# Ten smaller places for left operands and six raw places, from the first SwiGLU layer on

## The chip, the core and the metric

The kernel runs on one core of a Trainium2 chip. The time is the device time of one execution in microseconds. The engines that matter here are TensorE (PE in the profile, its weight loads PEld), VectorE (DVE), ScalarE (ACT), GpSimd (POOL) and SyncE (SP). Each follows its own list of instructions in order and waits on semaphores for the others. SP does nothing but issue transfers; POOL also issues some.

## The reference

```python
xn = _layernorm(x)                      # x: 1 x 2048 x 1024, float32
q, k, v = split_heads(xn @ wqkv)        # 32 heads of 32
pq, pk = phi(q), phi(k)                 # t + 1 where t > 0, else exp(t); + 1e-6
kv = einsum("bhsd,bhse->bhde", pk, v)
num = einsum("bhqd,bhde->bhqe", pq, kv)
den = einsum("bhqd,bhd->bhq", pq, pk.sum over s) + 1e-6
s = merge_heads(num / den) @ wo
h = silu(xn @ w1) * (xn @ w3)           # 2048 x 3584
g = silu(h @ w2)                        # w2: 3584 x 1024
return x + s * g
```

The change touches the two products at the end: the out-projection that gives `s`, and `h @ w2`, which is summed over 3584 columns of h.

## The kernel before, in words

Both products are done by blocks with seven products in place of eight (a Strassen form). Each float32 operand is split into a high part, rounded to the type that TensorE takes, and a low part, the rest. A product is then three matmuls: high by high (L103), high by low (L104) and low by high (L105). They are recorded at those lines whatever layer they belong to.

A `Segment` is one matrix product over all 2048 rows. Six of them run one after the other in the last third of the kernel: the attention's out-projection `s` (four k-steps), then five layers `B0` to `B4` that each take a part of the 3584 columns (`FB`: two k-steps in B0, three in the others; a k-step is 2 × 128 columns). Layers add to the accumulators `acc`, which stay in the on-chip memory; `uB` is a running sum that is stored in `u_d` between layers. In the last layer `finish` applies Silu (ACT, L1331), multiplies by `ss` (the attention's `s`, DVE, L1332), adds the input `xs` for some blocks (DVE, L1334) and stores the block.

A segment goes over eight row groups m = 0 to 7 of 256 rows. Each row group needs seven left operands, in this order: A11, S2, S3, S1, A12, A22, S4 (for the products B11, T2, T3, T1, B21, T4, B22). The left operands of the B layers lie in device memory in `h_d`. One goes through these steps:

- SP issues a load of its float32 form into a raw place (`left`, L1262 in the trace; the tile is called r..., for instance rS2B). A load is 128 KB in B0 and 192 KB in B1 to B4.
- ACT casts it to the high part of the operand's tile (XS2B, `split`, L95).
- DVE subtracts the high part from the raw form, which gives the low part (L96). After that the raw place is free for the next load.
- PE uses high and low part; after the last matmul that uses it, the operand's place is free.

The right operands (B11, T2 and so on, called B_k and T_k in the order of the program) are loaded and split by the same two lines L95 and L96 and kept for a whole layer. Their raw places are others.

In row groups m=1 to m=6 the kernel does one product after the other over all k-steps, in four banks of the matmul's accumulation memory (`aB` to `dB`). In m=0, and in m=7 if a layer follows, the k-steps are outermost and the seven products have a bank each, named for the product (B11B, T2B and so on), so that the right operands of the next layer can arrive k-step by k-step. At a seam between two layers, therefore, all seven left operands of m=7 are held until its end.

The order on each engine is made by a scheduler, from the program and from the places that a tile pool has; a pool with more places lets an operand's steps be put earlier. Before, all left operands of the attention and of the layers lie in pool `pb`, eight places of 4 KB per partition, and their raw forms in four places of 2 KB (tag `sg` of pool `pc`). Both pools live through the whole kernel. `era2` is a group of pools on the other (right) side of the memory that is closed when the attention is done; pool `pw`, with the right operands and the accumulators, opens in its room.

Of the kernel before, what the change touches and what calls it, by code (L numbers as in the profile page):

```python
# [9 lines left out]
F32 = mybir.dt.float32  # L10
FR = mybir.dt.float32r
# [5 lines left out]
P = 128  # L17
C = 512
# [4 lines left out]
def tile_linear_attention_times_swiglu(  # L23
# [67 lines left out]
    def split(pair, src, bias=None):  # L91

        hi, lo = pair[:, 0], pair[:, 1]
        if bias is None:
            nc.scalar.copy(out=hi, in_=src)  # L95
            return nc.vector.tensor_sub(out=lo, in0=src, in1=hi.bitcast(F32))  # L96
        nc.scalar.activation(hi, src, AF.Identity, bias=bias)
        return nc.vector.scalar_tensor_tensor(lo, src, bias, hi.bitcast(F32), op0=ALU.add, op1=ALU.subtract)
# [6 lines left out]
        return nc.tensor.matmul(acc, lhsT=wl, rhs=ah, start=False, stop=stop, skip_group_check=True)  # L105


    pb = ctx.enter_context(tc.tile_pool(name="pb", bufs=8))
    pe = ctx.enter_context(tc.tile_pool(name="pe", bufs=3))
    pc = ctx.enter_context(tc.tile_pool(name="pc", bufs=6))  # L110
    era1, era2 = ExitStack(), ExitStack()
    ctx.enter_context(tc.tile_pool(name="edge", bufs=1, side="right")).tile([P, 8], F32, name="edge")
    pa = era2.enter_context(tc.tile_pool(name="pa", bufs=1, side="right"))
    praw = era1.enter_context(tc.tile_pool(name="praw", bufs=2))
    st = era1.enter_context(tc.tile_pool(name="st", bufs=2))
# [2 lines left out]
        return pc.tile([P, C], F32, tag="c", name=name)  # L118

    def signed(name):  # L120
        return pc.tile([P, C], F32, tag="sg", bufs=4, name=name)

    def job_tile(shape, name):
        return praw.tile(shape, F32, tag="job", bufs=4, name=name)
# [66 lines left out]
    class Opening:  # L191
# [27 lines left out]
        def run(self):  # L219
            for step in OPENING.split(";"):  # L220
                name, *args = step.split()
                done = getattr(self, "do_" + name)(*args)
                if done is not None:
                    last = done
            return last
# [274 lines left out]
    def in_turn(groups):  # L500

        done = object()
        for g in groups:
            left = [o.stages for o in g]
            while left:
                for made in list(left):
                    if next(made, done) is done:
                        left.remove(made)
                    else:
                        yield  # L510
# [132 lines left out]
    def key_rows(h, pair):  # L643
# [7 lines left out]
        def steps(n, c, src):  # L651
            j = 2 * pair + n
            pk = signed(f"pk{h}_{j}_{c}")
            z = st.tile([P, 1], F32, tag="z", name="z")
            yield from phi_steps(src, pk, z)
            nc.vector.scalar_tensor_tensor(zacc[:, j:j + 1], z, C * 1e-6, zacc[:, j:j + 1],
                                           op0=ALU.add, op1=ALU.add)
            later.append([3, lambda: turn(n, c, pk)])
# [92 lines left out]
    def row_sums(i, m, b, u, v):  # L751
        V = nc.vector

        def keep(n, t):
            nc.gpsimd.dma_start(out=g_d[n][:, m], in_=t)

        if i == 0:
            u[m] = signed(f"gu{m}")
            nc.scalar.copy(out=u[m], in_=b)
        elif i == 2:  # L760
            V.tensor_add(out=u[m], in0=b, in1=u[m])
        elif i == 3:
            v[m] = pe.tile([P, C], F32, tag="u", name=f"gv{m}") if m else st.tile([P, C], F32, tag="own", bufs=1, name="gv")
            V.tensor_sub(out=v[m], in0=b, in1=u[m])
        else:
            c = small(f"gc{i}_{m}")
            if i == 1:
                nc.scalar.copy(out=c, in_=b)
            elif i == 4:
                V.tensor_sub(out=c, in0=v[m], in1=b)  # L770
            elif i == 5:
                V.tensor_add(out=c, in0=b, in1=u[m])
            else:
                V.tensor_sub(out=c, in0=v[m], in1=b)
            keep({1: 2, 4: 1, 5: 3, 6: 0}[i], c)

    def half(h):
# [13 lines left out]
        def queries(pair, **how):  # L791

            def use_q(n, c, src):
                j = 2 * pair + n
                pq = signed(f"pq{h}_{j}_{c}")
                phi(src, pq)
                nc.gpsimd.dma_start(out=pq_d[j // JG][2 * h + c][:, j % JG], in_=pq)  # L797

            return gemm(ops[f"q{h}_{pair}_"], A, use_q, **how)
# [327 lines left out]
    class Segment:  # L1127


        def __init__(self, name, nk, first, last, place, right, left, acc, end=None):  # L1130
            self.last, self.U = last, {}
            self.name, self.nk, self.first = name, nk, first
            self.place, self.right_of, self.left_of, self.acc, self.end = place, right, left, acc, end
            self.Y, self.X = {}, {}
# [9 lines left out]
        def operands(self, m):  # L1144

            self.X[m] = {}
            if not self.first:

                self.U[m] = pe.tile([P, C], F32, tag="u", name=f"u{self.name}_{m}")
                nc.sync.dma_start(out=self.U[m], in_=u_d[m])  # L1150
            for n, src in self.left_of(m):
                self.X[m][n] = pb.tile([P, 2, self.nk, P], FR, tag="b", name=f"X{n}{self.name}_{m}")
                split(self.X[m][n], src)

        def product(self, b, X, n, ks, start=True):
# [90 lines left out]
                take(c12, bd)  # L1246
                end(0, 1)

    loads = []

    def left(m, src, nk, name, first=False):

        big = None
        for e, n in enumerate(PRODUCTS):
            n = PARTNER[n]
            if first:
                if e % 2 == 0:
                    big = job_tile([P, 2, nk, P], f"r{e}{name}_{m}")
                t = big[:, e % 2]
            else:  # L1260
                t = signed(f"r{n}{name}_{m}")[:, :nk * P].rearrange("p (k s) -> p k s", s=P)
            loads[:] = [nc.sync.dma_start(out=t, in_=src(n))]  # L1262
            if name == "q" and m < 2:

                fetched[:] = loads
            yield n, t
# [15 lines left out]
    def second_weights(i, n, k):  # L1282
        if (i, n, k) not in asked:
            ask(i, n, k, small)
        return asked[i, n, k]
# [109 lines left out]
    def layer_place(n, i, k):  # L1395
# [4 lines left out]
                      lambda n, _, k, i=i: second_weights(i, n, k),  # L1400
# [6 lines left out]
            layers[0].right(0, [i for i in range(7) if i * 5 // 7 == m - 2])  # L1407

    run(attention, ahead=ask_next, around=first_weights)
    layers[0].operands(0)  # L1410
    era2.close()
    pw.append(ctx.enter_context(tc.tile_pool(name="pw", bufs=1, side="right", reuse_waits="tile")))
    for k in range(1, layers[0].nk):
        layers[0].right(k)
# [27 lines left out]
```

## Time and profile before

| | us |
|---|---|
| median of 3 runs | 2333.54 (2331.86 to 2333.63) |
| profiled execution | 2329.57 |
| its span | 2327.8 |
| PE busy in the span | 2288.8 (98%) |
| DVE busy | 1773.8 (76%) |
| ACT busy | 927.4 (40%) |
| POOL busy | 686.7 (30%) |
| last matmul of the attention starts | 1778.44 |
| first matmul of B0 starts | 1778.66 |

The profile is of one execution. Its times are microseconds from the span's start. Rows of a timeline give the start, the duration, the engine, the line, the operation, output and inputs, and in brackets the idle time of the engine ahead of it with what ended it. Matmuls are pipelined: each takes 0.39 us in the record, but the next one starts 0.23 us after it. The granted TensorE clock in the profiled execution is 0.999 of full speed.

### The profile page before, as it was taken

The page shows a single profiled execution, that of the slowest core. Times are in us where ns is not written, and L with a number is a line of the kernel's source. Part 1 is how long each engine was busy: PE and PEld are TensorE (multiplying, and loading weights), DVE is VectorE, ACT ScalarE, POOL GpSimd, SP SyncE. Part 2 cuts the span into 40 slices and gives each one's busy share as a digit, 9 for nine tenths or more (in the row PEclk, how much of TensorE's full clock was granted, in tenths as well). Part 3 has the DMA queues.
Part 4 walks back from the last instruction along what each step waited for, and adds up shares of the span by engine and source line. Part 5 has one row for each costly group of instructions (what it writes and reads, how often), then busy time and mean ns, then how long its engine had stood idle before and what let it go on. Part 6 is the DMA issues. An engine that isn't in the chain of part 4 may idle for free.

```text
span 2327.8 us, 31758 instructions
## 1 busy us (share of the span) xinstructions
PE 2288.8 (98%) x10752; PEld 1873.8 (80%) x10752; DVE 1773.8 (76%) x2820; ACT 927.4 (40%) x1645; POOL 686.7 (30%) x851
## 2 busy tenths in 40 slices
PE   6999999999999999999999999999999999999998
PEld 5888888888887888777887888888888888888876
DVE  8987888798877775657867788887655666776798
ACT  6555443433332555433333433234333624242433
POOL 3220524287766111001423334442310000000033
PEclk9999999999999999999999999999999999999999
DMA  6555556576669546786756666765755556665688
GB/s 235 163 190 176 185 164 199 163 240 199 225 223 339 199 136 213 263 253 200 228 181 188 193 200 208 208 207 176 235 179 185 183 175 187 223 205 180 193 267 261
DMA packets 353698, 478.69 MB, mean 206 GB/s; under 512 B 24208, under 2 KB 262800, under 8 KB 353424
## 3 DMA queue, kind: packets, MB, share of 16 engines
q1 hardware_dynamic: 315808, 356.58, 48.9%
q0 software_dynamic: 37728, 120.09, 15.8%
q8 instruction: 84, 1.38, 0.3%
q14 instruction: 78, 0.64, 0.1%
HBM read 305.66 MB, written 174.59 MB: 206 GB/s over the span
## 4 chain that ended last, share of the span: by engine, by line
PE 47%; issue 8%; DMA 5%; DVE 4%; POOL 3%; ACT 1%; SPq 0%; POOLq 0%; DVEq 0%; ACTq 0%
PE g L103 2%; PE g L104 2%; PE g L105 2%; PE cB L105 1%; PE dB L105 1%; PE dB L103 1%; PE dB L104 1%; PE cB L103 1%; PE cB L104 1%; PE aB L105 1%; PE aB L103 1%; PE aB L104 1%; DMA qs_d<-qd 1%; PE bB L103 1%; PE bB L105 1%
## 5 line engine op out<-in xcount | busy, mean ns | idle before, releaser
L871 POOL DMA_DIRECT2D h_d<-sg x112 | 82.9, 741 | 258.9 <-DVE sg L867 221.3
L1190 POOL DMA_DIRECT2D u_d<-uB x32 | 17.4, 542 | 402.6 <-DVE uB L1173 346.2
L96 DVE TENSOR_TENSOR xy<-xy,xy 128x512 fp32r<-128x512 f32 x112 | 73.0, 686 | 64.6 <-ACT xy L95 64.6
L95 ACT CAST xy<-xy 128x512 fp32r<-128x512 f32 x112 | 65.0, 620 | 102.1 <-PE g L105 60.6
L104 PE MATMUL g<-xy,xy 128*128 128x512 f32 x224 | 87.7, 392 | 0.5 <-DVE xy L96 0.4
L105 PE MATMUL g<-xy,xy 128*128 128x512 f32 x224 | 87.2, 390 | 0.0
L103 PE MATMUL g<-xy,xy 128*128 128x512 f32 x224 | 82.5, 397 | 0.0
L641 POOL DMA_DIRECT2D y_d<-y x48 | 34.9, 727 | 117.3 <-ACT y L665 71.0
L1173 DVE TENSOR_TENSOR acc<-cB,acc 128x512 f32<-128x512 f32 x50 | 34.4, 688 | 42.3 <-PE cB L105 42.2
L1173 DVE TENSOR_TENSOR acc<-dB,acc 128x512 f32<-128x512 f32 x56 | 38.6, 688 | 30.1 <-PE dB L105 29.9
L851 POOL TENSOR_TENSOR hs<-hs,sg 128x256 f32<-128x256 f32 x56 | 59.7, 1067 | 0.1
L853 POOL TENSOR_TENSOR hs<-sg 128x256 f32<-128x256 f32 x56 | 58.9, 1051 | 0.0
L103 PEld LDWEIGHTS g<-xy,xy 128*128 128x128 f32 x224 | 41.8, 188 | 14.0 <-issue 3.7
L1009 POOL DMA_DIRECT2D qs_d<-qd x32 | 18.1, 567 | 116.9 <-DVE qd L1005 77.5
L1304 POOL DMA_DIRECT2D s_d<-s x32 | 17.4, 543 | 118.9 <-DVE s L1173 70.1
L854 POOL TENSOR_TENSOR hs<-sg,hs 128x256 f32<-128x256 f32 x56 | 50.3, 899 | 1.5
L104 PEld LDWEIGHTS g<-xy,xy 128*128 128x128 f32 x224 | 42.0, 188 | 10.5 <-DVE xy L96 1.8
L850 POOL TENSOR_TENSOR hs<-sg,sg 128x256 f32<-128x256 f32 x56 | 49.6, 886 | 1.2
L105 PEld LDWEIGHTS g<-xy,xy 128*128 128x128 f32 x224 | 42.0, 188 | 8.9
L797 POOL DMA_DIRECT2D pq_d<-pq x32 | 17.6, 549 | 101.2 <-DVE pq L631 100.5
L879 POOL DMA_DIRECT2D h_d<-hs x60 | 46.4, 774 | 2.7 <-POOL hs L854 2.1
L95 ACT CAST XS4B<-rS4B 128x384 fp32r<-128x384 f32 (+1 forms) x40 | 19.7, 493 | 60.5 <-PE cB L105 41.1
(5325 smaller groups left out, 8287.3 us busy)
## 6 DMA issues: line engine op xcount, KB each, us to landing
h_d<-hs POOLq DMA_DIRECT2D x60, 256.0 KB, 3.5
h_d<-sg POOLq DMA_DIRECT2D x56, 256.0 KB, 4.2
w<-in_B_w SPq DMA_DIRECT2D x56, 256.0 KB
wt_d<-w SPq DMA_DIRECT2D x28, 512.0 KB
xy<-x_d SPq DMA_DIRECT2D x28, 512.0 KB
xy<-y_d SPq DMA_DIRECT2D x28, 512.0 KB
h_d<-hs SPq DMA_DIRECT2D x52, 256.0 KB
y_d<-y POOLq DMA_DIRECT2D x48, 256.0 KB, 3.8
```

The costliest lines, as they stand in the source:

```text
L95: nc.scalar.copy(out=hi, in_=src)
L96: return nc.vector.tensor_sub(out=lo, in0=src, in1=hi.bitcast(F32))
L103: nc.tensor.matmul(acc, lhsT=wh, rhs=ah, start=start, stop=False, skip_group_check=True)
L104: nc.tensor.matmul(acc, lhsT=wh, rhs=al, start=False, stop=False, skip_group_check=True)
L105: return nc.tensor.matmul(acc, lhsT=wl, rhs=ah, start=False, stop=stop, skip_group_check=True)
L850: e.tensor_add(out=s1, in0=a21, in1=a22)
L851: e.tensor_sub(out=s2, in0=s1, in1=a11)
L853: e.tensor_sub(out=s3, in0=a11, in1=a21)
L854: e.tensor_sub(out=s4, in0=a12, in1=s2)
L871: nc.gpsimd.dma_start(out=h_d[i][2 * h + c][:, 2 * n:4 * n + 2, k], in_=src)
L879: queue.dma_start(out=h_d[i][2 * h + c][:, 6 + 4 * e:10 + 4 * e, k], in_=o[e].rearrange("p (e s) -> p e s", s=P))
L1173: return V.tensor_add(out=c, in0=src, in1=c)
```

## The change

Left operands of the B layers get places of their own size. Pools `pb` and the four raw places (now a pool `psg`) become part of `era2`, on the right side. `era2` is closed as soon as the attention segment has been written down, before B0's first operands are asked for (before the change: after). In the room of 8 × 4 + 4 × 2 = 40 KB come `px`, ten places of 3 KB, `pr`, six places of 1.5 KB, and 1 KB of padding. They are opened with `reuse_waits="tile"`: a new tile waits for the tiles that lay in the same bytes. In B0 a tile of a left operand fills 2 KB of its 3 KB, in the other layers all of it.

```diff
-    pb = ctx.enter_context(tc.tile_pool(name="pb", bufs=8))
     pe = ctx.enter_context(tc.tile_pool(name="pe", bufs=3))
     pc = ctx.enter_context(tc.tile_pool(name="pc", bufs=6))
     era1, era2 = ExitStack(), ExitStack()
     ctx.enter_context(tc.tile_pool(name="edge", bufs=1, side="right")).tile([P, 8], F32, name="edge")
+    pb = era2.enter_context(tc.tile_pool(name="pb", bufs=8, side="right"))
+    psg = era2.enter_context(tc.tile_pool(name="psg", bufs=4, side="right"))
     pa = era2.enter_context(tc.tile_pool(name="pa", bufs=1, side="right"))
...
     def signed(name):
-        return pc.tile([P, C], F32, tag="sg", bufs=4, name=name)
+        return psg.tile([P, C], F32, tag="sg", name=name)
...
             for n, src in self.left_of(m):
-                self.X[m][n] = pb.tile([P, 2, self.nk, P], FR, tag="b", name=f"X{n}{self.name}_{m}")
+                self.X[m][n] = (px[0] if px else pb).tile([P, 2, self.nk, P], FR, tag="b", name=f"X{n}{self.name}_{m}")
                 split(self.X[m][n], src)
...
-    loads = []
+    loads, px = [], []
...
             else:
-                t = signed(f"r{n}{name}_{m}")[:, :nk * P].rearrange("p (k s) -> p k s", s=P)
+                t = px[1].tile([P, nk, P], F32, tag="r", name=f"r{n}{name}_{m}") if px else \
+                    signed(f"r{n}{name}_{m}").rearrange("p (k s) -> p k s", s=P)
             loads[:] = [nc.sync.dma_start(out=t, in_=src(n))]
...
     run(attention, ahead=ask_next, around=first_weights)
+    era2.close()
+    px.extend(ctx.enter_context(tc.tile_pool(name=n, bufs=b, side="right", reuse_waits="tile"))
+              for n, b in (("px", 10), ("pr", 6)))
+    ctx.enter_context(tc.tile_pool(name="pad", bufs=1, side="right")).tile([P, 2 * P], F32, name="pad")
     layers[0].operands(0)
-    era2.close()
     pw.append(ctx.enter_context(tc.tile_pool(name="pw", bufs=1, side="right", reuse_waits="tile")))
```

The same instructions run after the change as before, but in another order from the end of the attention on. Up to there the order is the same.

On DVE, at the seam between the attention and B0, the last additions of the attention (`us` and `s` from the banks as, bs, cs, ds) stood between the low parts of B0's first left operands. Before:

```order
L1180 TENSOR_TENSOR s_11_15171<-cs_15175,us_15172 128x512
L96 TENSOR_TENSOR XS1B_0_15289<-rS1B_0_15287,XS1B_0_15289 128x256
L1173 TENSOR_TENSOR s_11_15171<-ds_15176,s_11_15171 128x512
L96 TENSOR_TENSOR XA12B_0_15294<-rA12B_0_15292,XA12B_0_15294 128x256
L1236 COPY s_00_15168<-as_15173 128x512
L96 TENSOR_TENSOR XA22B_0_15299<-rA22B_0_15297,XA22B_0_15299 128x256
L1180 TENSOR_TENSOR s_10_15170<-cs_15175,us_15172 128x512
L96 TENSOR_TENSOR XS4B_0_15304<-rS4B_0_15302,XS4B_0_15304 128x256
L1180 TENSOR_TENSOR s_01_15169<-ds_15176,us_15172 128x512
```

Behind the change the additions come in a row, then four right operands of B0's second k-step, then the left operands:

```order
L1237 COPY s_00_15171<-as_15176 128x512
L1181 TENSOR_TENSOR s_10_15173<-cs_15178,us_15175 128x512
L1181 TENSOR_TENSOR s_01_15172<-ds_15179,us_15175 128x512
L96 TENSOR_TENSOR B_1_15326<-rB11B_1_15163,B_1_15326 128x512
L96 TENSOR_TENSOR T_1_15329<-rT2B_1_15165,T_1_15329 128x512
L96 TENSOR_TENSOR T_1_15332<-rT3B_1_15167,T_1_15332 128x512
L96 TENSOR_TENSOR T_1_15335<-rT1B_1_15169,T_1_15335 128x512
L96 TENSOR_TENSOR XA11B_0_15290<-rA11B_0_15288,XA11B_0_15290 128x256
L96 TENSOR_TENSOR XS2B_0_15295<-rS2B_0_15293,XS2B_0_15295 128x256
```

The low part of XA11 of B0's first row group has moved from behind the additions of attention's group m=6 to behind the last addition of m=7 and four right operands.

On PE, at the same seam, the first matmuls of B0 before:

```order
L105 MATMUL ds_15176<-wp_14133,XS4s_15048 128x512
L103 MATMUL B11B_0_15382<-B_0_14467,XA11B_0_15274 128x512
L104 MATMUL B11B_0_15382<-B_0_14467,XA11B_0_15274 128x512
L105 MATMUL B11B_0_15382<-B_0_14467,XA11B_0_15274 128x512
L103 MATMUL T2B_0_15383<-T_0_14472,XS2B_0_15279 128x512
```

And now:

```order
L105 MATMUL ds_15179<-wp_14136,XS4s_15051 128x512
L103 MATMUL B11B_0_15397<-B_0_14470,XA11B_0_15290 128x512
L104 MATMUL B11B_0_15397<-B_0_14470,XA11B_0_15290 128x512
L103 MATMUL T2B_0_15398<-T_0_14475,XS2B_0_15295 128x512
L104 MATMUL T2B_0_15398<-T_0_14475,XS2B_0_15295 128x512
L103 MATMUL T3B_0_15399<-T_0_14619,XS3B_0_15300 128x512
L104 MATMUL T3B_0_15399<-T_0_14619,XS3B_0_15300 128x512
L105 MATMUL B11B_0_15397<-B_0_14470,XA11B_0_15290 128x512
```

The matmul that needs the low part of XA11 (L105 on B11B) was the third of the layer and is now the seventh.

On SP, the loads at the start of B0, before:

```order
L1262 DMA rA22B_0_15297<-h_d_0_87 128x256
L1262 DMA rS4B_0_15302<-h_d_0_87 128x256
L1262 DMA rA11B_1_15346<-h_d_0_87 128x256
L1262 DMA rS2B_1_15351<-h_d_0_87 128x256
L1262 DMA rS3B_1_15356<-h_d_0_87 128x256
L1262 DMA rS1B_1_15361<-h_d_0_87 128x256
L1280 DMA rB21B_1_15323<-in_B_w 128x512
```

And now:

```order
L1264 DMA rA22B_0_15313<-h_d_0_87 128x256
L1282 DMA rB21B_1_15338<-in_B_w 128x512
L1282 DMA rT4B_1_15343<-wt_d_115 128x512
L1264 DMA rS4B_0_15318<-h_d_0_87 128x256
L1282 DMA rB22B_1_15348<-in_B_w 128x512
L1264 DMA rA11B_1_15361<-h_d_0_87 128x256
L1264 DMA rS2B_1_15366<-h_d_0_87 128x256
```

The load of rS4 has moved behind two right operands; the loads of the row group m=1 stand behind it and one right operand more.

## The prediction

> **What bounds the kernel now.** The page's head and its first part come first.
>
> ```profile
> span 2327.8 us, 31758 instructions
> PE 2288.8 (98%) x10752; PEld 1873.8 (80%) x10752; DVE 1773.8 (76%) x2820; ACT 927.4 (40%) x1645; POOL 686.7 (30%) x851
> ```
>
> TensorE (PE) is busy for 2288.8 of 2327.8 us, and the change takes away no matmul. All it can win is PE's gaps after the pools change hands, at 1778.66 us, where the attention segment ends and layer B0 begins. PE's waits from 1700 us to the end (engine, operation, line, what it waited for: total us, times, longest):
>
> ```profile
> PE cB L103 <- DVE acc L1173: 1.4, 1, 1.4
> PE aB L103 <- ACT XA11B L95: 1.1, 1, 1.1
> PE bB L103 <- ACT XS2B L95: 0.9, 1, 0.9
> PE cB L103 <- ACT XS3B L95: 0.5, 1, 0.5
> PE aB L105 <- DVE XA11B L96: 0.2, 1, 0.2
> ```
>
> Four of the five name a left operand (X...). None of them lies at a seam between two layers. PE's timeline shows the pace, and the wait in B0 at the passage from row group m=1 to m=2:
>
> ```profile
> 1778.44 0.39 PE L105 MATMUL ds<-wp,XS4s 128*128 128x512 f32 x1
> 1778.66 0.39 PE L103 MATMUL B11B<-B,XA11B 128*128 128x512 f32 x1
> 1783.20 0.39 PE L105 MATMUL B22B<-B,XS4B 128*128 128x512 f32 x1
> ...
> 1793.40 0.39 PE L105 MATMUL dB<-T,XS1B 128*128 128x512 f32 x1
> 1793.92 0.50 PE L103 MATMUL aB<-B,XA12B 128*128 128x512 f32 x1
> ...
> 1796.11 0.40 PE L104 MATMUL cB<-T,XA22B 128*128 128x512 f32 x1
> 1797.42 0.49 PE L103 MATMUL bB<-T,XS2B 128*128 128x512 f32 x1 [0.91 <-ACT XS2B L95]
> 1797.75 0.39 PE L104 MATMUL bB<-T,XS2B 128*128 128x512 f32 x1
> ```
>
> From 1778.66 to 1783.20 are 20 steps, the three matmuls of seven products: 0.227 us each. A wait costs more than its bracket says: 1796.11 to 1797.42 is 1.31, or 1.08 over one step, and the next step (1797.42 to 1797.75) is 0.10 too long; together 1.18 against 0.91 shown. So I add 0.27 to each shown wait. With 1793.40 to 1793.92 (0.29 over, and 0.11 by the same restart) this place loses 1.58 us.
>
> The last layer's waits, by the same timeline:
>
> ```profile
> 2239.21 0.50 PE L103 MATMUL aB<-B,XA11B 128*128 128x512 f32 x1 [1.07 <-ACT XA11B L95]
> 2240.91 0.50 PE L103 MATMUL cB<-T,XS3B 128*128 128x512 f32 x1 [0.47 <-ACT XS3B L95]
> 2241.59 0.50 PE L105 MATMUL aB<-B,XA11B 128*128 128x512 f32 x1 [0.18 <-DVE XA11B L96]
> 2273.58 0.50 PE L103 MATMUL cB<-T,XA22B 128*128 128x512 f32 x1 [1.40 <-DVE acc L1173]
> ```
>
> With 0.27 each: 1.34 + 0.74 + 0.45 = 2.53 us for left operands, 1.67 us for an accumulation. All that can be recovered is 1.58 + 2.53 + 1.67 = 5.78 us.
>
> The chain of waits tells why the last layer is late (start, us, what the time went to); these rows of it are one ring, a load, its cast on ScalarE (ACT), its low part on VectorE (DVE), the next load into the same raw place:
>
> ```profile
> 2226.34 7.99 DMA rA22B<-h_d
> 2234.43 0.52 ACT XA22B L95
> 2234.98 0.57 DVE XA22B L96
> 2235.57 4.68 DMA rS3B<-h_d
> ...
> 2285.23 5.16 DMA rS4B<-h_d
> ```
>
> From rA22 at 2226.34 to rS4 at 2285.23 the chain goes through eight loads, each four operands after the one before: 28 operands in 58.89 us, 2.10 us each. PE needs 9 × 0.227 = 2.04 us for one (three matmuls for each of three k-steps). Four raw places are just too few here.
>
> **The change part by part.** No operand's arithmetic, cast or byte of traffic is added; every engine runs the same instructions, in another order from the seam on.
>
> *First use of the new pools.* This is the cost. Before, the first layer's left operands took free places of the old pool, and their low parts ran on DVE between the attention's last additions. Now the places lie where operands of attention's last group still are. In the new order six low parts of B0's m=0 stand behind the last addition and four weight low parts. DVE before, with one row of the last layer:
>
> ```profile
> 1776.75 0.42 DVE L96 TENSOR_TENSOR XS4B<-rS4B,XS4B 128x256 fp32r<-128x256 f32 x1
> 1778.86 0.69 DVE L1180 TENSOR_TENSOR s<-ds,us 128x512 f32<-128x512 f32 x1 [1.70 <-PE ds L105]
> 1779.47 0.68 DVE L96 TENSOR_TENSOR B<-rB11B,B 128x512 fp32r<-128x512 f32 x1
> 1781.28 0.69 DVE L96 TENSOR_TENSOR T<-rT1B,T 128x512 fp32r<-128x512 f32 x1
> 1781.88 0.42 DVE L96 TENSOR_TENSOR XA11B<-rA11B,XA11B 128x256 fp32r<-128x256 f32 x1
> 1782.21 0.69 DVE L96 TENSOR_TENSOR B<-rB21B,B 128x512 fp32r<-128x512 f32 x1
> ...
> 2240.99 0.55 DVE L96 TENSOR_TENSOR XA11B<-rA11B,XA11B 128x384 fp32r<-128x384 f32 x1
> ```
>
> The addition starts 0.42 after the last attention matmul; the four weight parts follow from 1779.47, and at 1781.88, where m=1's XA11 stood, comes m=0's. It ends at 1782.30, and PE takes it 0.05 later (as 2240.99 + 0.55 is followed by 2241.59 in the last layer). PE's first matmul on it (B11 L105) now stands seventh, so its slot is 1778.66 + 6 × 0.227 = 1780.02. Wait: 1782.35 − 1780.02 = 2.33, with the restart of 0.10: **+2.43 us**. The other low parts follow 0.33 apart (1781.88 to 1782.21), while PE spends three or four matmuls, 0.68 us or more, between them: no second wait. The high parts: XS3's place comes free with attention's last matmul, its cast can run from 1778.86 for 0.41, and PE wants it at 1778.66 + 4 × 0.227 = 1779.57: 0.3 us to spare.
>
> The seventh load, rS4, has only six places and waits for XA11's low part, about 1782.36; queued behind it on SP are the last k=1 weight and all of m=1's loads. The nearest load rows:
>
> ```profile
> 1792.93 0.38 SPq L1262 DMA_DIRECT2D rS2B<-h_d  x1
> 1796.96 0.41 ACT L95 CAST XS2B<-rS2B 128x256 fp32r<-128x256 f32 x1 [1.77 <-DMA rS2B<-h_d]
> ```
>
> 4.03 us to the cast, 0.41 for it: XS4 is ready at 1786.8. Its first matmul is the 35th in the new order: 1778.66 + 34 × 0.227 + 2.43 = 1788.8, so it is hidden, for any load below about 6 us. Cost 0; the far bound, the 7.99 above, makes it 2.0.
>
> *Six raw places instead of four.* In B0 the late rS2 was issued 1792.93, when a place came free; with two more it goes out two operands earlier, and two operands are 2 × 6 × 0.227 = 2.7 us there, against 1.58 lost. I take all: **−1.58** (bounds 0 and −1.58; 0 if the m=1 loads stay behind rS4).
>
> In the last layer a lap of the ring takes 4 × 2.10 = 8.4 us; over six places it is 1.40 us per operand, well under PE's 2.04. I take all of **−2.53** (bounds 0 and −2.53). [...] The rows say 4.68 to 7.99 for loads that SP issues, so the sum goes by the rows.
>
> *DVE's share.* Whether faster loads help depends on DVE (columns: sum of the stretch, then busy us of PE, PE loads, DVE, ACT, POOL; clock, DMA share, GB/s):
>
> ```profile
> 1850.00:1900.00 50.00, 50.00 (x222) 41.41 (x221) 37.74 (x67) 21.89 (x44) 2.17 (x4) 1.00 0.71 220
> 2200.00:2250.00 50.00, 48.29 (x211) 38.96 (x210) 46.79 (x77) 20.32 (x40) 12.79 (x13) 1.00 0.79 246
> 2250.00:2300.00 50.00, 48.58 (x213) 39.57 (x212) 48.38 (x82) 20.17 (x40) 18.46 (x20) 1.00 1.04 322
> ```
>
> DVE is busy 95.17 of the last layer's 100 us shown. The accumulation that PE awaits at 2273.58 is late because DVE has a backlog, and part of that comes from late operands. I take half of 1.67: **−0.84** (bounds 0 and −1.67). The tail after the last matmul is DVE's too; 0.
>
> *Ten left places instead of eight.* Between layers, three operands of the next layer's m=0 instead of one stand ahead of its weights on DVE: two more, 0.55 us each at most. The row from 1850 to 1900 holds such a seam and PE loses nothing in it (50.00 of 50.00), with DVE at 37.74: 0 at four seams.
>
> *Sum*: 2.43 − 1.58 − 2.53 − 0.84 = **−2.52 us**. The profiled execution took 2329.57 us (span 2327.8 and 1.8 around it), which gives 2327.05. The median of the runs is 2333.54 (2331.86 to 2333.63), 4.0 above the profiled one; with the same difference I predict **2331.0 us**. 0.2%, about what a measurement of this kernel tells from no change, is 4.7 us.
>
> **The rivals.**
>
> *(a) The last layer does not speed up.* It would be bound by DVE (95%), or by the transfers: 322 GB/s and a DMA share of 1.04 in the stretch from 2250, against 220 and 0.71 earlier. Two more places give a head start only once; then loads come no faster than the engines move them. For it: PE still waits there with everything queued. Against it: in the stretch from 2200, where the operand waits lie, DMA share is 0.79. The last layer gives 0, and the sum is 2.43 − 1.58 = +0.85, or 2334.4. [...]
>
> *(b) Slower: every layer seam pays as the first one does.* The order is new at all four, and DVE is the engine that PE would wait for: two operands stand ahead of the weight parts there. If each costs between the B0 wait of 1.18 and the first seam's 2.43, that is +4.7 to +9.7 on the sum, −2.52: 2335.7 to 2340.7. It decides from 2.52/4 = 0.63 us per seam. Against: no wait at any seam before, and the row at 1850 leaves DVE 12 us free. A late rS4 (up to 2.0, with the 1.58 lost: +3.6) would alone give 2334.6.
>
> *(c) More is recovered.* The whole accumulation wait goes (−0.83 more) and the first seam's wait is hidden by half (−1.2): −4.5, 2329.0. For it: a DVE without late operands. Against: the order at the seam leaves nothing to hide behind.
>
> **How the numbers follow.** My case, with its bounds of the halved term and small misses, 2329.5 to 2332.5: 0.48. Rival (a), whole or in part: 0.22. Rival (b): 0.20. Rival (c): 0.10. The range for 8 in 10: low end 2328.0, below (c); high end 2338.2, the middle of (b). Faster by over 0.2% (below 2328.9) needs more than (c): 0.07. Slower by over 0.2% (above 2338.2) needs the upper half of (b), or a wait I don't see: 0.14. Within: 0.79.
>
> **What would show it.** A PE wait on DVE XA11B (L96) at B0's start, about 2.1 to 2.3 us as shown; none at m=1 to m=2; in the last layer no PE wait on ACT XA11B or XS3B, with the chain no longer going through four-place laps of loads; a remaining wait on an accumulation of under 1.4 us. I am wrong if PE waits at a layer seam, if XS4 of B0's m=0 comes late, or if DVE's busy share in the last layer rises to 100% while PE's waits just change their names.

## The result, and the profile after

The changed kernel takes 2329.07 us (median of 15 runs, 2325.63 to 2330.50), the kernel before 2332.43 us (median of 15 runs beside it). The ratio is 0.9983, with a 95% interval of 0.9976 to 0.9990: 3.4 us faster by the medians, inside the 0.2% that was called no change. The forecast was 2.5 us less than before, and 2331.0 us.

The page of the changed kernel has these lines:

```profile
span 2327.3 us, 31735 instructions
PE 2292.7 (99%) x10752; PEld 1879.2 (81%) x10752; DVE 1772.8 (76%) x2820; ACT 925.8 (40%) x1645; POOL 686.2 (29%) x851
```

Its profiled execution took 2329.09 us. Of the five waits of PE after 1700 us none is left, and there is one new one:

```profile
PE B11B L105 <- DVE XA11B L96: 2.2, 1, 2.2
```

PE's timeline at the seam between the attention and B0:

```profile
1780.53 0.39 PE L105 MATMUL ds<-wp,XS4s 128*128 128x512 f32 x1
1780.75 0.39 PE L103 MATMUL B11B<-B,XA11B 128*128 128x512 f32 x1
...
1781.88 0.39 PE L104 MATMUL T3B<-T,XS3B 128*128 128x512 f32 x1
1784.44 0.50 PE L105 MATMUL B11B<-B,XA11B 128*128 128x512 f32 x1 [2.17 <-DVE XA11B L96]
1784.78 0.40 PE L103 MATMUL B11B<-B,XA11B 128*128 128x512 f32 x1
...
1786.87 0.63 PE L105 MATMUL T2B<-T,XS2B 128*128 128x512 f32 x1
1787.30 0.63 PE L103 MATMUL T1B<-T,XS1B 128*128 128x512 f32 x1
```

The seventh matmul of B0 comes 2.33 us late (2.56 from 1781.88, less one step of 0.227), and the restart costs 0.11. A second loss was not foreseen: from about 1785.3 to 1788.7, at a granted clock of 0.50, the matmuls start 0.43 us apart instead of 0.23. After that no step from one matmul to the next is more than 0.05 us too long, to the end of the kernel.

DVE and ACT show what the wait was for:

```profile
1780.95 0.69 DVE L1181 TENSOR_TENSOR s<-ds,us 128x512 f32<-128x512 f32 x1 [2.03 <-PE ds L105]
1781.56 0.68 DVE L96 TENSOR_TENSOR B<-rB11B,B 128x512 fp32r<-128x512 f32 x1
...
1783.36 0.69 DVE L96 TENSOR_TENSOR T<-rT1B,T 128x512 fp32r<-128x512 f32 x1
1783.96 0.42 DVE L96 TENSOR_TENSOR XA11B<-rA11B,XA11B 128x256 fp32r<-128x256 f32 x1
```

```profile
1772.84 0.40 ACT L95 CAST XA11B<-rA11B 128x256 fp32r<-128x256 f32 x1
...
1780.99 0.41 ACT L95 CAST XS3B<-rS3B 128x256 fp32r<-128x256 f32 x1 [7.45 <-issue]
```

XA11 was cast at 1772.84, so its place and its data were there; DVE was idle for 2.03 us right ahead of 1780.95. But in its list the low part stood behind that addition and four right operands, and so it ran at 1783.96, eleven microseconds after the cast. The stretches of the last layer (columns as before), in which PE now does not lose anything:

```profile
2200.00:2250.00 50.00, 50.00 (x222) 41.24 (x221) 50.00 (x83) 23.24 (x46) 13.70 (x13) 1.00 0.84 257
2250.00:2300.00 50.00, 50.00 (x222) 41.41 (x221) 49.87 (x86) 20.61 (x42) 22.62 (x21) 1.00 1.06 341
```

From B0's first matmul to the end of the span it is 546.58 us now and 549.14 before: 2.56 less. Ahead of it the order is the same, but this execution is 2.09 us later there; it ran two stretches at half clock, at 48 and at 748 us, that the profiled execution of before did not have.

### The profile page after: what moved, and what is told of

It reads as the page before. It is cut to its first block, busy times and chain, and to the rows that moved or that the text cites. A ratio compares the mean times of both kernels' runs of the same rounds, so it can differ in the third digit from the quotient of the medians.

```text
span 2327.3 us, 31735 instructions
## 1 busy us (share of the span) xinstructions
PE 2292.7 (99%) x10752; PEld 1879.2 (81%) x10752; DVE 1772.8 (76%) x2820; ACT 925.8 (40%) x1645; POOL 686.2 (29%) x851
## 4 chain that ended last, share of the span: by engine, by line
PE 63%; DVE 3%; DMA 1%; issue 1%; ACT 1%; SPq 0%; DVEq 0%; ACTq 0%
PE g L103 2%; PE g L104 2%; PE g L105 2%; PE aB L103 2%; PE aB L104 2%; PE aB L105 2%; PE dB L103 2%; PE dB L104 2%; PE cB L103 2%; PE cB L104 2%; PE dB L105 2%; PE cB L105 2%; PE bB L103 1%; PE bB L104 1%; PE bB L105 1%
## 5 line engine op out<-in xcount | busy, mean ns | idle before, releaser
L105 PE MATMUL g<-xy,xy 128*128 128x512 f32 x224 | 87.2, 390 | 0.0
L105 PEld LDWEIGHTS g<-xy,xy 128*128 128x128 f32 x224 | 42.0, 188 | 8.9
L887 POOL TENSOR_TENSOR w<-w 128x256 f32<-128x256 f32 x28 | 26.8, 956 | 50.3 <-DMA w<-in_B_w 50.3
```

## The experiments

All times below are ratios to the kernel before, run on the same chip, with 95% intervals; medians are in us. The ratio on record is not the quotient of the two medians, and where the two tell different things both are given.

**The move of the pools alone.** The new pools get the old numbers of places.

```diff
-              for n, b in (("px", 10), ("pr", 6)))
-    ctx.enter_context(tc.tile_pool(name="pad", bufs=1, side="right")).tile([P, 2 * P], F32, name="pad")
+              for n, b in (("px", 8), ("pr", 4)))
+    ctx.enter_context(tc.tile_pool(name="pad", bufs=1, side="right")).tile([P, 2560], F32, name="pad")
```

> The new pools with the old numbers of places: eight left places of 3 KB, four raw places of 1.5 KB. My theory (the move of the pools costs at the seam, the raw places pay in the last layer): the wait of PE at B0's start for the low part of XA11 stays at about 2.2 us, a second one of about 0.8 us comes for XA12, whose raw place is the fifth of four, and the waits of the kernel before in the last layer (1.1 and 0.5 us for operands, 1.4 us for an accumulation) are back. Against the kernel before +2.4 and +1.0 to 1.3, less nothing: 3 to 5 us longer, ratio 1.0013 to 1.0022. Rival (the seam's wait is paid back later by something that the move itself brings): within 1 us of before.

Measured: 1.0019 (1.0009 to 1.0028), 2336.00 against 2331.28. PE's waits after 1700 us:

```profile
PE B11B L105 <- DVE XA11B L96: 2.1, 1, 2.1
PE cB L103 <- DVE acc L1174: 1.2, 1, 1.2
PE aB L103 <- ACT XA11B L95: 1.0, 1, 1.0
PE cB L103 <- ACT XA22B L95: 0.9, 1, 0.9
PE bB L105 <- DVE XS2B L96: 0.7, 1, 0.7
PE cB L103 <- ACT XS3B L95: 0.5, 1, 0.5
PE aB L105 <- DVE XA11B L96: 0.2, 1, 0.2
```

The seam's wait and all waits of the last layer stand side by side, so the move by itself brings nothing back and is a pure cost: 4.7 us by the medians, as forecast. The wait that was expected for XA12 at the seam did not come; B0 paid later instead, for XS2 and XA22 (0.7 and 0.9). The seam's wait was also followed by slow matmuls in this profile (granted clock 0.50 from 1783.59 to 1787.00, see the half clock below).

**Six raw places, eight left places.** As above with `("px", 8), ("pr", 6)` and the padding made up.

> Eight left places, six raw places. My theory (the ring of raw places is what held the last layer): no operand wait in B0 at m=1 to m=2 nor in the last layer, the seam's wait of 2.2 us as in the changed kernel, time within 1 us of the changed kernel, about 3 us under before (ratio 0.998 to 0.9995). Rival (the two added left places do it): the last layer's waits of 1.1 and 0.5 us are back, 2 to 5 us over before.

Measured: 0.9988 (0.9978 to 0.9997), 2329.26 against 2331.28. The waits:

```profile
PE B11B L105 <- DVE XA11B L96: 2.1, 1, 2.1
PE dB L103 <- ACT XS1B L95: 0.3, 1, 0.3
```

The two raw places alone clear the last layer, and nearly all of B0.

**Ten left places, four raw places.** As above with `("px", 10), ("pr", 4)`.

> Ten left places, four raw places. My theory: as the run with the old numbers, seam's wait 2.2 us and one of about 0.8 us for XA12, the last layer's operand waits back, 3 to 5 us over before (ratio 1.0013 to 1.0022). Rival (left places do it): last layer without operand waits, about 3 us under before, as the changed kernel.

Measured: 1.0017 (1.0008 to 1.0026), 2333.84 against 2331.28. The ratio is as my theory had it (by the medians it is 2.6 us, a little under the 3 expected), but not the waits:

```profile
PE B11B L105 <- DVE XA11B L96: 2.1, 1, 2.1
PE cB L103 <- ACT XA22B L95: 1.1, 1, 1.1
PE dB L103 <- DVE acc L1174: 1.1, 1, 1.1
PE bB L103 <- ACT XS2B L95: 1.1, 1, 1.1
PE cB L103 <- DVE acc L1174: 0.9, 1, 0.9
```

The waits on XA22 and XS2 are in B0. In the last layer the operand waits are gone, and two accumulation waits stand in their place. DVE's timeline shows the second:

```profile
2262.66 0.56 DVE L96 TENSOR_TENSOR XA22B<-rA22B,XA22B 128x384 fp32r<-128x384 f32 x1 [1.02 <-ACT XA22B L95]
2263.20 0.69 DVE L1334 TENSOR_TENSOR acc<-acc,ss 128x512 f32<-128x512 f32 x1
2263.81 0.68 DVE L1174 TENSOR_TENSOR acc<-dB,acc 128x512 f32<-128x512 f32 x1
```

DVE stands for 1.02 us in front of a low part whose load is late, and behind it in its list stands the accumulation that PE waits for. With more left places the scheduler puts low parts earlier in DVE's list; a late load then holds up other work. An accumulation wait can be a load wait under another name.

**Three low parts first.** The changed kernel, with an edge on DVE alone: the low parts of the right operands of B0's later k-step come after those of XA11, XS2 and XS3. (`low` collects the low parts that `split` returns; `issue_after` sets an order on the engine of the given instruction.)

```diff
...
-                split(self.X[m][n], src)
+                self.low.append(split(self.X[m][n], src))
...
-    for k in range(1, layers[0].nk):
-        layers[0].right(k)
+    with tc.issue_after(layers[0].low[2].ins):
+        for k in range(1, layers[0].nk):
+            layers[0].right(k)
```

> The changed kernel, with the low parts of the first three left operands of B0 put ahead of the low parts of the right operands of its second k-step on DVE. My theory (the seam's wait is the order on DVE, 2.4 us, and the half clock behind it, 1.6 us where it comes): XA11's low part ends at 0.37 us past PE's slot, the wait shown there is under 0.4 us in place of 2.17, and the time is 2 to 4 us under the changed kernel, about 5 to 7 us under before (ratio 0.997 to 0.998). Rival (PE waits there for the transfers or for ScalarE, the order is no matter): the wait stays at about 2 us or comes a few matmuls later, time as the changed kernel.

Measured: 0.9982 (0.9973 to 0.9991), 2326.08 against 2331.28. The wait shown at the seam is 0.21 us. The ratio lies just above the expected 0.997 to 0.998, and its interval covers most of that range; by the medians it is 5.2 us, within the 5 to 7 expected. To set it against the changed kernel, both ran again on one chip.

> The changed kernel once more, beside the next three on one chip. Seam's wait 2.15 to 2.2 us shown, no other wait after it; 2.5 to 4 us under before. [...]

> Changed kernel with three low parts of B0's left operands ahead of four right operands' on DVE, again, for the comparison with the changed kernel on the same chip: 2 to 3.5 us under it by the medians (2.0 of wait, and 0.9 for the half clock that comes in about half of its executions and not here).

Measured: the changed kernel 0.9983 (0.9974 to 0.9992), 2327.54; with three low parts first 0.9976 (0.9967 to 0.9984), 2326.67. That is 0.9 us by the medians, not 2 to 3.5, and the intervals overlap. The waits of the latter show a part of the reason:

```profile
PE bB L103 <- ACT XS2B L95: 0.6, 1, 0.6
PE B11B L105 <- DVE XA11B L96: 0.2, 1, 0.2
```

B0 comes to XS2 of its third row group before the load is there. The seam does not hold PE up any more, and this load also goes out later: 12.6 us after B0's first matmul, against 11.4 in the changed kernel's profile beside it. All steps over 0.05 us too long, added up, are 2.7 us in that execution of the changed kernel and 1.5 us in this one. The stop at XS2 is not the same every time: with its restart it costs 0.9 us here and 0.4 in the first profile of the same kernel. In that execution of the changed kernel the seam brought no half clock. So the trace shows the seam's wait gone, but the times do not show that as much is won.

**Five raw places**, with three low parts first.

> As the run with three low parts first, but five raw places instead of six. By the ring: a lap of 8.4 us over five places is 1.7 us per operand, under PE's 2.04, so the last layer stays without operand waits, and only the start of B0 can pay (the sixth left operand waits for a place): within 1.5 us of the run with six. Rival (DVE is the limit of the last layer and the reserve counts): accumulation waits of over 1 us come back in the last layer, 2 us or more.

Measured: 0.9991 (0.9982 to 1.0000), 2329.89, against 2326.67 with six on the same chip: 3.2 us more where at most 1.5 were expected. The waits:

```profile
PE cB L103 <- ACT acc L1182: 0.9, 1, 0.9
PE bB L103 <- ACT XS2B L95: 0.6, 1, 0.6
PE dB L105 <- DVE XS1B L96: 0.6, 1, 0.6
PE B11B L105 <- DVE XA11B L96: 0.2, 1, 0.2
```

The last layer is as free as with six, as expected, and the rival's waits did not come. All of it falls in B0, between 1793 and 1805 us: there an operand feeds PE for only 6 × 0.227 = 1.36 us. The loads issued there show how long a raw place takes from one load to its next, for instance the place of XS1, which goes to the fifth operand after it:

```profile
1789.73 0.63 SPq L1264 DMA_DIRECT2D rS1B<-h_d  x1
1798.65 0.45 SPq L1264 DMA_DIRECT2D rS2B<-h_d  x1
```

Five laps in a row from 1787.83 on take 7.2 to 8.9 us, which over five places is 1.4 to 1.8 us per operand: more than 1.36. With six places the laps there are 7.1 to 7.6 us, 1.2 to 1.3 us per operand. The longest wait, on an addition of ACT (L1182), is a late load as well: just ahead of it ACT was idle for 1.29 us until the load of XS4 was there.

**Eight left places, six raw places**, with three low parts first.

> As the run with three low parts first, but eight left places instead of ten, six raw places. Theory (raw places alone do it): within 1 us of ten left places, perhaps a wait of 0.3 us in B0 as in the run with eight and six before. Rival (the two more left places matter at the layer seams or in the last layer): over 2 us longer.

Measured: 0.9980 (0.9971 to 0.9989), 2327.18, 0.5 us above ten left places and no more than the noise. With six raw places the ninth and tenth left place bring nothing that these runs can tell. With four they brought 2.2 us by the medians (2336.00 to 2333.84 above), but there the ratios, 1.0019 and 1.0017, are not apart.

**Ten raw places, eight left places**, with three low parts first: the room of the two left places goes to raw places.

```diff
-              for n, b in (("px", 10), ("pr", 6)))
+              for n, b in (("px", 8), ("pr", 10)))
```

> Eight left places, ten raw places, three low parts first: the room of two left places goes to raw places. Theory (raw places are what both B0 and the last layer lacked): the seam's wait stays at 0.2 us shown, the wait of 0.3 to 0.6 us for XS2 in B0 goes, the last layer stays free of waits; 0.5 to 1 us under the run with ten and six, about 5.5 us under before (ratio 0.9972 to 0.998). Rival (ten raw loads at once crowd the transfers, or loads run too early and hold back right operands and ss): a new wait of PE on a right operand at a seam or on ACT's cast of one, 1 us or more over the run with six.

> [...]

Measured: ten raw places 0.9971 (0.9959 to 0.9983), 2325.66; the changed kernel, run a third time beside it, 0.9984 (0.9975 to 0.9992), 2328.92; before 2332.76. It has the lowest ratio of all, though its interval overlaps those of the runs with six raw places, so a gain over these is not shown by the times. The trace shows what was expected: after 1700 us the 0.21 us at the seam is its only wait, it loses 0.5 us in all, and the rival's wait on a right operand did not come.

**The half clock.** In the changed kernel's first profile the granted clock is 0.50 in three stretches between the start and the last matmul. Each lasts 3.41 us; they begin at 47.93, 747.66 and 1785.32 us, which is 205 and 304 times 3.413 us apart. In the other executions that show such a stretch it lasted 3.41 us too, or twice that (from 746.01 with three low parts first, from 46.33 with five raw places), and where two came, they began 304 times 3.413 us apart (745.94 and 1783.59, the move alone) or 205 times (47.18 and 746.92 with eight and six; 48.60 and 748.33 with eight and six and three low parts first). Cut into stretches of 3.413 us, counted from such a start, the changed kernel's first profile reads (stretch, length, busy us of PE and the others, then clock):

```profile
1778.49:1781.90 3.41, 3.41 (x17) 2.81 (x15) 1.38 (x3) 0.91 (x3) 0.54 (x1) 1.00 0.57 145
1781.90:1785.32 3.42, 1.25 (x6) 0.75 (x5) 3.42 (x9) 0.42 (x2) 0.54 (x1) 1.00 0.35 109
1785.32:1788.73 3.41, 3.41 (x10) 2.64 (x9) 2.51 (x7) 2.45 (x5) 0.00 (x0) 0.50 0.87 253
```

and the third profile of the same kernel, with the same wait of 2.17 us:

```profile
1782.06:1785.47 3.41, 2.13 (x10) 1.44 (x8) 2.60 (x5) 1.33 (x4) 0.54 (x1) 1.00 0.75 209
1785.47:1788.88 3.41, 2.52 (x11) 2.10 (x12) 2.67 (x8) 1.29 (x3) 0.00 (x0) 1.00 0.47 151
```

There the wait lies in one stretch (PE busy 1.25 of 3.42), here in two (1.28 and 0.89 idle): half clock there, none here. The wait's length, 2.17 us in both, did not tell the two apart.

The clock also fell to 0.50 behind the last matmul: in the changed kernel at 2321.21 us, 157 times 3.413 us after 1785.32. Where an execution shows no other half-clock stretch, the stretches are counted back from there. In the kernel before, the fall is at 2322.39, and a wait of 2.98 us, up to 47.48, lies in two:

```profile
42.29:45.70 3.41, 2.21 (x14) 1.68 (x12) 3.41 (x3) 3.40 (x6) 3.27 (x5) 1.00 0.91 347
45.70:49.12 3.42, 1.64 (x11) 1.47 (x12) 3.42 (x6) 1.77 (x4) 0.47 (x1) 1.00 0.48 193
```

That is 1.20 and 1.78 us idle, and no half clock; in the changed kernel 2.78 us of the same wait fell into one stretch, and one came at 47.93. In the changed kernel's second profile (fall at 2319.02) the seam's wait, 2.17 us again, lies in two as well, but most of it in one:

```profile
1779.70:1783.12 3.42, 1.49 (x7) 0.91 (x5) 3.25 (x6) 1.33 (x4) 0.54 (x1) 1.00 0.74 176
```

With 1.93 us idle there no half clock came.

The waits of 2.15 to 2.17 us at the seam brought a half-clock stretch in three of six profiles: in the changed kernel's first, with the move alone and with ten and four, but not with eight and six nor in the changed kernel's second and third.

## Why the prediction was right

The time was 1.9 us below the predicted one and inside the range; before, too, ran 1.1 us lower in the larger set of runs. Term by term, from the two first profiles (each wait with its restart):

| step | forecast | measured |
|---|---|---|
| seam, XA11's low part | +2.43 | +2.44 |
| half clock behind it | not in the sum | +1.61 in this execution |
| B0, m=1 to m=2 | −1.58 | −1.58 |
| last layer, operands | −2.53 | −2.53 |
| last layer, accumulation | −0.84 | −1.67 |
| a short stop of 0.28 at 2260 before | not in the sum | −0.28 |
| from the last matmul's start to the end | 0 | −0.32 |
| sum | −2.52 | −2.33 |

The profile has −2.56 from B0's start; the other 0.23 is in steps too small to list. That this total comes so near to the forecast is in part luck: the 1.61 us that the sum lacked are made up by 0.83 more from the accumulation, 0.28, 0.32 and these 0.23.

*First use of the pools.* The wait, its place, its size and its releaser came out as worked out, as did the spare time of XS3's cast, and the late rS4 was hidden. What was wrong is the reason given for XA11: "the places lie where operands of attention's last group still are". XA11's cast at 1772.84 shows its place free long before. (For XS3 it may hold: its cast starts 0.46 us behind the attention's last matmul, as worked out, though the profile names no releaser.) Built with the raw pool put ahead of the left pool, or with the padding first, so that other bytes lie beneath each tile, the kernel has the same order of instructions on DVE, row for row. So the order does not come from what lies beneath a tile; why the scheduler makes it was not looked into. The run with three low parts first shows that order alone made the wait.

*What the sum lacked* is the half clock: 1.6 us more in three of six profiles with this wait, and in one of three of the changed kernel. The prediction does not reckon with the clock. The profile of before gave no hint of it: there a wait of 2.98 us, up to 47.48, was followed by a granted clock of 1.00.

*Six raw places.* Right, as a mechanism (four and six at eight left places: the last layer's waits return and go) and in size. But the count behind it was wrong. From rA22 at 2226.34 to rS4 at 2285.23 SP issues 30 loads of left operands, so 29 steps, not 28: 2.03 us each (a lap of 8.1 us, not 8.4), no more than PE's 2.04. The chain's loads are three, four or five operands apart, because it passes from one raw place to another in DVE's list. An average over so many laps cannot show a shortage, as the ring can't run ahead of PE for long. What shows it are the single laps at PE's waits from 2239 to 2242, this one for the XA11 that PE waits for:

```profile
2230.57 0.40 SPq L1262 DMA_DIRECT2D rA11B<-h_d  x1
2241.57 0.34 SPq L1262 DMA_DIRECT2D rA12B<-h_d  x1
```

Four places on, the same raw place gets its next load 11.0 us later, which is 2.75 us per operand; the two laps that begin before this one take 9.2 and 9.1 us, the next one 11.0. The run with the move alone, with four places as well, has the last layer's operand waits back (1.0, 0.5 and 0.2 us).

*DVE's share.* The accumulation wait was mis-sized: not half of it went but all, 1.67. It was taken partly for DVE's own load. The run with six raw and eight left places has it gone, so the raw places took it away. In the kernel before, too, late loads stand ahead of that addition in DVE's list:

```profile
2266.49 0.56 DVE L96 TENSOR_TENSOR XA11B<-rA11B,XA11B 128x384 fp32r<-128x384 f32 x1 [0.58 <-ACT XA11B L95]
2270.16 1.55 DVE L96 TENSOR_TENSOR XS3B<-rS3B,XS3B 128x384 fp32r<-128x384 f32 x1 [0.25 <-ACT XS3B L95]
```

Both casts had waited for their load. These two stops are 0.83 us against the 1.40 of the wait; XS3's low part also took 1.55 us instead of 0.55, and why is open.

*Rival (a)*, a last layer bound by DVE or the transfers, did not come: DVE is busy for 99.87 of 100 us there now, at 341 GB/s in the second half, and PE loses nothing. DVE's share did rise to nearly 100%, which the prediction had named as a sign of being wrong, but only if PE's waits changed their names, and they are gone. PE has no gap left there that faster operands could close. *Rival (b)* did not come either: at the four layer seams PE has no wait, in any profile. *Rival (c)* had the accumulation right and the seam wrong.

## What to carry to other kernels

Count a ring of buffers by its lap: load, cast, low part and the wait for the next issue, over the number of places, against what one operand feeds the slowest engine. Read the laps from the rows of the stretch where that engine waits; an average over a whole layer only gives the engine's own pace back. Split a change of pools into its numbers and its move: the gain was in the raw places, the left places gave nothing that the runs can tell with six raw ones, and the move cost 2.4 us at the seam, which an order edge took away. Where an accumulation is late, look at what stands ahead of it in the engine's list before calling the engine full.

## What the runs showed of the hardware

In the twelve profiles, each cut into stretches of 3.413 us as above, from 15 us after the start to the last matmul, a stretch at full clock with 2.04 to 2.87 us without a matmul was followed by one at a clock of 0.50 in all twelve cases, one with 1.64 to 1.93 us in three of twelve (1.91 with eight and six, 1.80 and 1.64 in the two runs with three low parts first), and one with less in none. What sets these three apart from the other nine was not shown. Two half-clock stretches with 0.92 us (three low parts first) and 0.96 us (five raw places) without a matmul were followed by a second one; the others had at most 0.20 us and were not. In the changed kernel's first profile the half-clock stretch behind the seam, full of matmuls, cost 1.61 us. The seam's wait of 2.17 us so cost 4.05 us there, 2.44 of it without the half clock; in the second and third profile of the same kernel, with the same wait, no half clock followed.
